# A planner that sorts TensorE's work by when its operands are ready, plus a slack: two attention and two feed-forward layers on one core

## The chip, the cores and the metric

The kernel runs on one core of a Trainium2 chip. The metric is device time in microseconds (us) of one execution, as the median of several. A core has five engines that work in parallel, each through its own list of instructions in order: TensorE (PE, matrix products), VectorE (DVE), ScalarE (ACT), GpSimd (POOL) and SyncE (SP, which here only issues transfers). They wait for each other through semaphores.

## The reference: what is computed

x has 2048 tokens of 640 features. The two layers A and B are each applied twice, A, B, A, B, every time as x = x + layer(layernorm(x)):

```python
# A: 32 heads of 20 features; the tokens in 4 segments of 512, one after the other
q, k, v = x @ wq, x @ wk, x @ wv
p     = softmax(q_s k_s^T * scale + causal mask)      # within segment s
a_mem = phi(q_s) M / (phi(q_s) z + 1e-6)              # M, z: of the segments before
o     = g * a_mem + (1 - g) * (p v_s)
M, z += phi(k_s)^T v_s, sum(phi(k_s))                 # phi(t) = t + 1 if t > 0 else exp(t)
out   = o @ wo
# B
out   = relu(x @ w1) @ w2                             # 640 -> 1728 -> 640
```

The segments of A follow each other through M and z. B works on each token alone, so B of one segment can run beside A of another.

## The kernel before, in words

**Tiling.** All work goes by segments (a, s): a is the first or second pair of layers, s one of the four segments. For each segment TensorE does the following, one 128x128 tile of weights at a time:

- `proj_part` and `proj_v` make q, k and v from the normalised, transposed tokens xnT, by matmuls of 512 or 320 columns (recorded under lines L598 and L601 of the helper `group`, which all whole-array matmuls of projections and B share).
- q and k are copied from PSUM to `stg`, spilled to a scratch tensor in HBM (`spill`, L859) and read back in another layout as `pad`, four heads at 32 partitions' distance (`fill`, L906, four transfers for each pair of head groups).
- `scores` (L1078) multiplies q and k of four heads at once in row tiles of 32 partitions. It goes by rounds: one round fills two two-bank slots of PSUM, ACT takes the exponentials of both (`exps`, L1140, 128x1024 each), which frees the slots. POOL cuts the triangle (`causal`, L1152).
- `apply` (L1172) multiplies the result PT by v in column tiles of 32, copies it to `otu`, transposes it by a transfer (`turn_pair`, into `otk`), and DVE divides (`divide`). `mem_read` (L969) and `mem_write` (L1021) read and update M; the latter needs the transposed phi(k), `phk`, again through a transfer.
- `turn_o` transposes the sum of both parts into `oT`, `out_proj` multiplies by wo, and DVE adds the result to x (`add_half`, L1294). `ln_b` normalises and transposes again, and `ffn` and `ffn_rest` (L1352) do layer B.

All transposes by transfer are issued by `turn` (L631). Spills, fills, transposes and output stores share SP's one list. The results of the whole-array matmuls go through four PSUM banks (`MISC`); `evac` copies them out on ACT or DVE, whichever the planner finds free first.

**What sets the order.** No order is written out by hand. Each step above is a Python generator, a *stream*, that yields one operation (`Op`) after the other: the engine or engines that may do it, an estimate of its time on each, what it waits for, and the buffer that it acquires. `Sched.run` plans the program while it is built. It keeps an estimated time at which each engine is free (`free`) and at which each result is ready (`t`, read through `at`). In each step it looks at the head of every stream, and takes the one with the smallest key:

```python
key = (round(start + late), 0.5 if op.urgent else prio, self.rank[id(st[1])], n)
```

`start` is the estimated start: the later of the engine being free and of every operand being ready, plus `SEM_NS` (60) and, on TensorE, `PE_MARGIN` (80). `late` comes from `_late`. Before the change it is 0 except for operations with a `lag` (the column-tiled `apply` and `ffn_rest`, `COLS_LAG` 1500 ns). Ties go by priority (scores and exponentials first, B last) and then by the segment. Score rounds come to the planner as an `Either`; for them `run` sets `late` to 0.0 itself and doesn't call `_late`:

```python
both, lone = st[2].fn()
if both is not None:
    heads.append((st[0], n, st, self._alts(both), both, 0.0))
```

The chosen operation is appended to its engine's list for good. So on the chip every engine works through a fixed list, and if an operand is late the engine stands, whatever else lies further down. The estimates decide the order alone; the waits are real semaphores.

A transfer's estimated landing is its issue, plus bytes by a rate on one shared DMA clock (`dma_free`), plus a latency: `turn` uses 2400 ns and 270 bytes a ns, a spill 2300, a fill 1500 with 130 bytes a ns.

Of the kernel before, what the change touches and what calls it, by code (L numbers as in the profile page):

```python
# [38 lines left out]
class Prog:  # L39
    def __init__(self, sems):  # L40
        self.ops = {e: [] for e in ENGS}
        self.clk = dict(sems)
        self.cnt = {e: 0 for e in ["act", "dve", "pool", "pe"]}
        self.dcnt = {}
        self.K = {e: {} for e in ENGS}
        self.pos = {e: 0 for e in ENGS}
        self.info = {}
# [109 lines left out]
LONE_NS = 300.0  # L157
SWITCH_NS = 96.0
COLS_LAG = 1500.0
SEM_NS = 60.0  # L160
PE_MARGIN = 80.0
HOLDERS = 1
# [3 lines left out]
class Sched:  # L166


    def __init__(self, prog):
        self.P = prog  # L170
        self.free = {e: 800.0 for e in ENGS}
        self.t = {}
        self.events = {}
        self.streams = []
        self.dma_free = 0.0
        self.rank = {}
        self.mode = "full"

    def add(self, prio, gen):
        self.streams.append([prio, gen, None, None, False])  # L180
        self.rank[id(gen)] = 0
# [4 lines left out]
    def set(self, *key, tks=()):  # L186
        assert key not in self.events, key
        self.events[key] = [t for t in tks if t is not None]
# [35 lines left out]
    def _alts(self, op):  # L224
# [7 lines left out]
        for k, (e, hold, fns, tail) in enumerate(op.alts):  # L232
            m = PE_MARGIN if e == "pe" else 0.0
            if e == "pe" and op.mode != self.mode:
                hold = hold + SWITCH_NS
            start = max([self.at(t) + SEM_NS + m for t in waits], default=0.0)
            start = max(self.free[e], start)
# [3 lines left out]
        return res  # L241

    def _late(self, op):
        if not op.lag or self.mode != "full":
            return 0.0
        waits = op.waits
        if op.acq is not None:
            s = self._pick(op.acq)
            waits = waits + (s.tks if s is not None else [])
        ready = max([self.at(t) for t in waits], default=0.0) + SEM_NS + PE_MARGIN  # L250
        return max(0.0, ready + op.lag - max(ready, self.free["pe"]))

    def run(self):
        while True:
            best = None
            moved = True
            while moved:
                moved = False
                for st in self.streams:
                    had, ended = st[2], st[4]  # L260
                    self._settle(st)
                    moved = moved or st[4] != ended
                    moved = moved or st[2] is not had
            heads = []
            for n, st in enumerate(self.streams):
                if st[4]:
                    continue
                if isinstance(st[2], Op):
                    heads.append((st[0], n, st, self._alts(st[2]), st[2], self._late(st[2])))
                elif isinstance(st[2], Either):  # L270
# [3 lines that stand above are left out]
                    if lone is not None:  # L274
                        heads.append((8, n, st, self._alts(lone), lone, LONE_NS))
            for prio, n, st, alts, op, late in heads:
                ok = []
                for end, start, k, e in alts:
                    if not any(p2 < min(prio, HOLDERS) and st2 is not st
                               and any(e2 == e and s2 + HOLD_TOL[e] < end for _, s2, _, e2 in al2[:1])  # L280
                               for p2, _, st2, al2, _, _ in heads):
                        ok.append((end, start, k))
                if not ok:
                    continue
                end, start, k = min(ok)
                key = (round(start + late), 0.5 if op.urgent else prio, self.rank[id(st[1])], n)
                if best is None or key < best[0]:
                    best = (key, st, end, start, k, op)
            if best is None:
                stuck = [st for st in self.streams if not st[4]]  # L290
                if not stuck:
                    return
                raise RuntimeError("stuck: " + "; ".join(
                    str(getattr(st[2], "key", None) or [s.name for s in getattr(st[2], "slots", [])][:2]) for st in stuck))
            _, st, end, start, k, op = best
            e, hold, fns, tail = op.alts[k]
            if e == "pe":
                self.mode = op.mode
            waits, slot = op.waits, None
            for s in op.take:  # L300
                s.free = False
            if op.acq is not None:
                slot = self._pick(op.acq)
                slot.free = False
                waits = waits + slot.tks
                fns = [(lambda eng, fn=fn, slot=slot: fn(eng, slot), mark) for fn, mark in fns]
            self.P.waits(e, waits)
            self.free[e] = end
            if op.dma is not None:
                tk = self.P.dma(e, fns[0][0], op.dma)  # L310
                self.dma_free = max(self.dma_free, start + 300.0) + tail[1]
                self.t[(id(tk[0]), tk[1])] = max(self.dma_free, end) + tail[0]
                if tail[2]:
                    self.free[e] = max(end, self.dma_free)
                out = tk
            else:
                marks = []
                for fn, mark in fns:
                    tk = self.P.op(e, fn, mark)
                    if tk is not None:  # L320
                        self.t[(id(tk[0]), tk[1])] = end + tail
                        marks.append(tk)
                out = marks[0] if len(marks) == 1 else (marks or None)
            st[2], st[3] = None, ((slot, out) if slot is not None else out,)


def pe(ns, fns, waits=(), acq=None, take=(), mode="full", lag=0.0):
    return Op([("pe", ns, fns, 190.0)], waits, acq=acq, take=take, mode=mode, lag=lag)
# [18 lines left out]
def evac(n, mode, vfn, afn, waits=(), psum=True):  # L347
    return Op([("act", (60.0 if psum else 94.0) + n / 1.2, [(afn, True)], 125.0),
               ("dve", 66.0 + n / (0.96 * mode), [(vfn, True)], 95.0)], waits, urgent=True)
# [12 lines left out]
def bass_interleave_layers__memory_aug_infini_attn__dense_activation_relu__prompt_kernel(  # L362
    nc, A_x, A_wq, A_wk, A_wv, A_wo, A_beta, B_x, B_w1, B_w2, out,
):
    with contextlib.ExitStack() as es:
# [794 lines left out]
        def apply(n):  # L1160
# [9 lines left out]
            for j in range(NJ):  # L1170
                for hh in range(4):
# [3 lines left out]
                        j == NJ - 1 and hh == 3))  # L1175
            OD, tk = yield pe(540.0, fns, mk + vt, acq=MISC, mode="cols", lag=COLS_LAG)
            pt.release(tk)
# [164 lines left out]
        def ffn_rest(b, s):  # L1342
# [6 lines left out]
            for k in range(FC):  # L1349
                for z in range(2):  # L1350
                    for c in range(2):
# [4 lines left out]
                            start=(k == 0), stop=(k == FC - 1)), k == FC - 1 and z == 1 and c == 1))  # L1356
            bk, tk = yield pe(550.0, fns, xtk + w1t, acq=MISC, mode="cols", lag=COLS_LAG)
            th = yield evac(256, 1, lambda e: e.tensor_scalar(hR[:], bk.ap[:, 0:L // 2], 0.0, None, ALU.max),
# [141 lines left out]
```

## Time and profile before

| | |
|---|---|
| median of 8 runs | 567.72 us (566.27 to 570.42) |
| the profiled execution: its own time | 569.41 us |
| the profiled execution: span of its instructions | 567.7 us |
| TensorE (PE) busy | 554.2 us, 98% |
| VectorE (DVE) busy | 412.9 us, 73% |
| ScalarE (ACT) busy | 406.4 us, 72% |
| GpSimd (POOL) busy | 192.4 us, 34% |
| exponentials, L1140 | 320 of 1025 ns |
| granted TensorE clock | full speed in every slice |

The page is of one execution. Its span runs from the first instruction to the last, and its time (569.41) has 1.7 us around that. "Busy" is the union of the instructions' records on an engine. A matmul's record includes its way through the pipeline, so matmuls overlap in the records, and the time from one start to the next is the better measure of what one costs. "Idle before" is the engine's gap before an instruction, and behind the arrow stands what ended it. The chain of waits is followed back from the last instruction through whatever released each one. PEld are the loads of weights, which run beside matmuls.

### The profile page before, as it was taken

How to read it: one execution, taken by the hardware profiler on the slowest of the kernel's cores; microseconds unless marked ns; L12 is line 12 of the kernel's file. 1: busy time of each engine (PE TensorE's matmuls, PEld its weight loads, DVE VectorE, ACT ScalarE, POOL GpSimd, SP SyncE). 2: the span in 40 equal slices, each digit the busy share in tenths (PEclk: the TensorE clock that was granted, in tenths of full speed). 3: DMA queues.
4: the chain of work that ended last, by engine and by line, in shares of the span. 5: the costliest groups of instructions: out<-in, count | busy, mean ns of one | idle time of the engine just before them, and what ended most of it. 6: DMA issues, size and time to landing. Idle time of an engine off the chain costs nothing.

```text
span 567.7 us, 12814 instructions
## 1 busy us (share of the span) xinstructions
PE 554.2 (98%) x5212; PEld 297.0 (52%) x5212; DVE 412.9 (73%) x1064; ACT 406.4 (72%) x512; POOL 192.4 (34%) x302
## 2 busy tenths in 40 slices
PE   7998999999999999999999999999999999999998
PEld 6554554445454545645445545564444553665655
DVE  5957898977989799877587985599856875562202
ACT  5699879889778878978898776688777777213140
POOL 5346344343444344344333442044331433100000
PEclk9999999999999999999999999999999999999999
DMA  8695998835374428472288122861429510432101
GB/s 267 145 219 160 209 210 182 228 70 103 91 140 89 86 57 164 98 106 43 83 156 143 21 51 53 207 99 26 62 74 174 110 44 18 90 69 52 44 0 47
DMA packets 129980, 60.92 MB, mean 107 GB/s; under 512 B 108802, under 2 KB 119810, under 8 KB 129922
## 3 DMA queue, kind: packets, MB, share of 16 engines
q1 hardware_dynamic: 129504, 59.62, 48.9%
q8 instruction: 41, 0.67, 0.5%
q10 hardware_dynamic: 418, 0.49, 0.3%
q14 instruction: 17, 0.14, 0.1%
HBM read 20.57 MB, written 12.85 MB: 59 GB/s over the span
## 4 chain that ended last, share of the span: by engine, by line
PE 76%; DVE 11%; DMA 8%; ACT 2%; SPq 1%; POOL 1%; issue 1%; ACTq 0%
PE ps L601 49%; PE ps L598 10%; PE ps L1078 7%; PE ps L1172 5%; DMA otk<-otu 3%; DVE stats L609 2%; ACT PT L1140 1%; DVE hT L1379 1%; PE ps L1021 1%; PE ps L969 1%; PE ps L1211 1%; DMA pad<-scr 1%; DMA oT<-o_sb 1%; DMA phk<-phs 1%; DVE o_sb L1266 1%; SPq L906 1%
## 5 line engine op out<-in xcount | busy, mean ns | idle before, releaser
L1140 ACT ACTIVATE PT<-ps 128x1024 bf16<-128x1024 f32 x320 | 308.9, 1025 | 69.0 <-PE ps L1078 66.3
L1152 POOL TENSOR_SCALAR_AFFINE_SELECT PT<-PT 128x512 bf16<-128x512 bf16 x256 | 167.0, 671 | 271.4 <-ACT PT L1140 271.3
L601 PE MATMUL ps<-w_r,hT 128*128 128x320 bf16 x768 | 123.5, 299 | 0.0
L601 PE MATMUL ps<-xnT,w_r 128*128 128x512 bf16 x416 | 114.6, 379 | 0.0
L1294 DVE TENSOR_TENSOR x_sb<-x_sb,ps 128x320 bf16<-128x320 bf16 x128 | 60.7, 481 | 69.5 <-PE ps L601 68.9
L601 PEld LDWEIGHTS ps<-w_r,hT 128*128 128x128 bf16 x768 | 72.9, 98 | 33.1 <-issue 5.6
L1078 PE MATMUL ps<-pad 20*128 20x512 bf16 (+3 forms) x1024 | 63.4, 301 | 2.5 <-DMA pad<-scr 1.2
L601 PEld LDWEIGHTS ps<-xnT,w_r 128*128 128x128 bf16 x416 | 39.6, 98 | 42.2 <-issue 3.4
L609 DVE BATCH_NORM_STATS2 stats<-x_sb 128x6 f32<-128x320 bf16 x124 | 55.3, 469 | 2.8 <-DMA x_sb<-in_A_x_dram 2.6
L1379 DVE TENSOR_SCALAR hT<-ps 128x512 bf16<-128x512 f32 x54 | 36.8, 682 | 13.0 <-PE ps L601 12.8
L601 PE MATMUL ps<-wo_r,oT 128*128 128x320 bf16 x256 | 46.2, 299 | 0.0
L1078 PEld LDWEIGHTS ps<-pad 20*128 20x128 bf16 x1024 | 17.9, 92 | 53.1 <-ACT PT L1140 26.5
L1381 ACT ACTIVATE hT<-ps 128x512 bf16<-128x512 f32 x50 | 29.9, 598 | 21.9 <-PE ps L601 21.6
L1172 PE MATMUL ps<-PT,v_aug 128*21 128x128 bf16 (+3 forms) x896 | 40.5, 301 | 0.0
L598 PE MATMUL ps<-xnT,w_r 128*128 128x512 bf16 x104 | 39.6, 381 | 0.3 <-DVE om_sb L980 0.3
L1182 DVE CAST otu<-ps 128x512 bf16<-128x512 f32 x49 | 33.4, 682 | 7.3 <-PE ps L1172 7.1
L601 PE MATMUL ps<-wv_r,xnT 128*128 128x320 bf16 x192 | 36.3, 300 | 0.0
L625 POOL TENSOR_TENSOR rstd<-lnU,mhalf 128x2 f32<-128x2 f32 (+2 forms) x26 | 20.4, 783 | 44.3 <-DVE lnU L621 42.2
L935 ACT ACTIVATE stg<-stg 128x512 bf16<-128x512 bf16 x50 | 31.6, 632 | 4.6 <-DVE rtmp L933 4.4
L601 PE MATMUL ps<-xnT,wk_r 128*128 128x512 bf16 (+1 forms) x128 | 34.8, 366 | 0.0
L601 PE MATMUL ps<-xnT,wq_r 128*128 128x512 bf16 (+1 forms) x128 | 33.6, 366 | 0.0
L655 DVE TENSOR_SCALAR xn_tok<-x_sb,mv,rstd 128x640 bf16<-128x640 bf16 x60 | 30.3, 538 | 2.0 <-POOL rstd L625 1.7
(108 smaller groups left out, 672.0 us busy)
## 6 DMA issues: line engine op xcount, KB each, us to landing
pad<-scr SPq DMA_DIRECT2D x124, 80.0 KB
scr<-stg SPq DMA_DIRECT2D x34, 256.0 KB, 3.3
out_dram<-x_sb SPq DMA_DIRECT2D x16, 160.0 KB, 1.8
w_r<-in_B_w_dram SPq DMA_DIRECT2D x10, 216.0 KB, 2.6
w_r<-in_B_w_dram SPq DMA_DIRECT2D x13, 160.0 KB, 2.8
x_sb<-in_A_x_dram SPq DMA_DIRECT2D x10, 160.0 KB, 3.4
scr<-w_r SPq DMA_DIRECT2D x5, 256.0 KB, 3.3
wv_r<-in_A_wv_dram SPq DMA_DIRECT2D x1, 800.0 KB, 8.7
```

The costliest lines, as they stand in the source:

```text
L598: bk, tk = yield pe(mm_ns(n), [(lambda e, bk, a=a, b=b: e.matmul(bk.ap[:, 0:n] if len(b.shape) == 2 else bk.ap[:, 0:n].rearrange("p (i n) ...
L601: tk = yield pe(mm_ns(n), [(lambda e, k=k, a=a, b=b, bk=bk: e.matmul(bk.ap[:, 0:n] if len(b.shape) == 2 else bk.ap[:, 0:n].rearrange("p (i ...
L609: tk = yield dve(320, 1, lambda e, c2=c2: e.bn_stats(stats6[:, t % 12, c2, :], x_sb[:, t, c2 * 320:(c2 + 1) * 320]), xt)
L655: nm = lambda e, bx, t, k: e.tensor_scalar(bx.ap[:, k * D:k * D + D], x_sb[:, t + k, :], mv[:, t + k, 0:1], rstd[:, t + k:t + k + 1], ALU. ...
L935: te = yield act(512, lambda e, q=q: e.activation(q, q, ACT.Exp), [tr] + p, psum=False)
L1078: fns.append([(lambda e, z=z, j=j, hh=hh, N=N, o=o, sl=sl, q=hh % 2: e.matmul(slot.ap[:, q, o:o + N], sl.ap[32 * hh:32 * hh + DH, z, 0, 12 ...
L1140: tx = yield act(1024, lambda e, dst=dst, src=src: e.activation(dst, src, ACT.Exp, scale=SCALE), sc + pw)
L1152: tm = yield pool(600.0, lambda e, reg=reg: e.affine_select(out=reg, in_=reg, pattern=[[0, 4], [1, 128]], compare_op=ALU.is_ge, fill=0.0, ...
L1172: fns.append((lambda e, OD, j=j, hh=hh: e.matmul(OD.ap[32 * hh:32 * hh + DH + 1, 128 * j:L], VAUG[vx(a, s)][:, j, 4 * g + hh, :], pt.ap[:, ...
L1182: te = yield evac(L, 1, lambda e: e.tensor_copy(dst, OD.ap), lambda e: e.activation(dst, OD.ap, ACT.Copy), [tk] + OTU[0].tks)
L1294: ta = yield dve(320, 1, lambda e: e.tensor_tensor(x_sb[:, t, 320 * hf:320 * hf + 320], x_sb[:, t, 320 * hf:320 * hf + 320], bk.ap[:, 0:32 ...
L1379: th = yield evac(512, 1, lambda e, dc=dc, bk=bk: e.tensor_scalar(hT[:, dc, :], bk.ap[:, :], 0.0, None, ALU.max), lambda e, dc=dc, bk=bk: ...
```

## The change

Three constants are new, and `_late` gets a part for TensorE. It is at work from the point at which the event `("sc",6,4,1)` has been set: the planner has placed the last score round of the seventh pair of head groups, in the second segment of the first layer A. For each operand of the operation (and of the buffer that it would acquire), the estimated time at which it is ready is taken, plus the two margins, plus a slack: 400 ns (`SOFT`) if an engine makes it, 1000 ns (`SOFT_DMA`) if a transfer brings it. If that lies behind the estimated start, the difference is the lateness. It goes into the sort key alone: an operation whose operands have just become ready sorts as if it started later, so others with older operands come first. It isn't kept waiting if there is nothing else, and the start that the planner books is the same. Operations with a `lag` get the larger of both. A set `landed` remembers which results come by a transfer. No instruction, wait, buffer or estimate is changed.

```diff
@@ -157,6 +157,9 @@
 LONE_NS = 300.0
 SWITCH_NS = 96.0
 COLS_LAG = 1500.0
+SOFT = 400
+SOFT_DMA = 1000
+SOFT_FROM = ("sc",6,4,1)
 SEM_NS = 60.0
 PE_MARGIN = 80.0
 HOLDERS = 1
@@ -175,6 +178,7 @@
         self.dma_free = 0.0
         self.rank = {}
         self.mode = "full"
+        self.landed = set()
 
     def add(self, prio, gen):
         self.streams.append([prio, gen, None, None, False])
@@ -241,14 +245,24 @@
         return res
 
     def _late(self, op):
+        late = 0.0
+        if op.alts[0][0] == "pe" and SOFT_FROM in self.events:
+            waits = op.waits
+            if op.acq is not None:
+                s = self._pick(op.acq)
+                waits = waits + (s.tks if s is not None else [])
+            start = max([self.free["pe"]] + [self.at(t) + SEM_NS + PE_MARGIN for t in waits])
+            for t in waits:
+                k = (id(t[0]), t[1])
+                late = max(late, self.t[k] + SEM_NS + PE_MARGIN + (SOFT_DMA if k in self.landed else SOFT) - start)
         if not op.lag or self.mode != "full":
-            return 0.0
+            return late
         waits = op.waits
         if op.acq is not None:
             s = self._pick(op.acq)
             waits = waits + (s.tks if s is not None else [])
         ready = max([self.at(t) for t in waits], default=0.0) + SEM_NS + PE_MARGIN
-        return max(0.0, ready + op.lag - max(ready, self.free["pe"]))
+        return max(late, ready + op.lag - max(ready, self.free["pe"]))
 
     def run(self):
         while True:
@@ -308,6 +322,7 @@
             self.free[e] = end
             if op.dma is not None:
                 tk = self.P.dma(e, fns[0][0], op.dma)
+                self.landed.add((id(tk[0]), tk[1]))
                 self.dma_free = max(self.dma_free, start + 300.0) + tail[1]
                 self.t[(id(tk[0]), tk[1])] = max(self.dma_free, end) + tail[0]
                 if tail[2]:
```

## The prediction, made before the result was known

> **What bounds the kernel now.** I read the page's busy line first, then its chain, then busy time in three stretches of the span, then TensorE's own waits, and last the timeline around the waits. The busy line and the chain say that TensorE is the bound:
>
> ```profile
> PE 554.2 (98%) x5212; PEld 297.0 (52%) x5212; DVE 412.9 (73%) x1064; ACT 406.4 (72%) x512; POOL 192.4 (34%) x302
> ...
> PE 76%; DVE 11%; DMA 8%; ACT 2%; SPq 1%; POOL 1%; issue 1%; ACTq 0%
> ```
>
> TensorE's order in the two built programs is the same for its first 516 pieces of work, up to the apply at 111.6 us. So the change can act only behind that point. The stretches (us busy, instructions):
>
> ```profile
> 0.00:111.60 111.60, 105.53 (x1169) 58.10 (x1170) 89.82 (x247) 92.18 (x124) 48.55 (x85) 1.00 0.83 203
> 111.60:450.00 338.40, 333.80 (x3161) 172.75 (x3155) 273.49 (x701) 270.21 (x331) 127.08 (x191) 1.00 0.49 97
> 450.00:567.70 117.70, 114.89 (x892) 66.13 (x890) 49.61 (x118) 44.04 (x59) 16.77 (x26) 1.00 0.20 48
> ```
>
> The columns are length, then PE, PEld, DVE, ACT, POOL, the clock (1.00 throughout) and DMA. In the middle stretch DVE (273.5) and ACT (270.2) stand at 81% and 80% of 338.4; they have room, TensorE has none. Its waits there:
>
> ```profile
> PE ps L1078 <- DMA pad<-scr: 1.2, 1, 1.2
> PE ps L598 <- DMA oT<-o_sb: 1.1, 1, 1.1
> PE ps L598 <- DMA xnT<-xn_tok: 0.8, 1, 0.8
> PE ps L1021 <- DMA phk<-phs: 0.4, 1, 0.4
> ```
>
> These gaps run from a modelled end, and a matmul's record is longer than its place in the pipeline, so they understate the loss. I count from start to start instead:
>
> ```profile
> 398.77 1.03 PE L601 MATMUL ps<-xnT,w_r 128*128 128x512 bf16 x4
> 400.62 0.31 PE L598 MATMUL ps<-wv_r,xnT 128*128 128x320 bf16 x1 [0.82 <-DMA xnT<-xn_tok]
> ```
>
> Four matmuls of 0.38 us cover 1.03, so they start (1.03 - 0.38)/3 = 0.216 apart. The next should have started at 398.77 + 4 x 0.216 = 399.63 and started at 400.62: 0.99 us lost, not 0.82. The same median steps over the trace are 0.136 for 320 columns, 0.230 for a score round, 0.558 for an apply by columns, and 0.098 more at each change between whole-array, row-tile and column-tile matmuls. They sum to 551.8 us of TensorE work. From the first matmul's start (1.59) to the last one's is 563.05. So 11.3 us are lost to waiting: 4.1 before 111.6 us, **7.2 behind it**. That 7.2 is all the change can win.
>
> It is made of 4.05 for transfers (1.30 pad at 432.07, 1.26 oT at 250.88, 0.99 xnT, 0.50 phk at 294.07), 2.36 in twelve waits of 0.07 to 0.50 for DVE or ACT (0.65 of it four score rounds waiting for L1140), and 0.78 in pieces under 0.06.
>
> [...]during the 0.99 us above no other matmul ran, though work was at hand; so where an operand is late, the place in the list is all that matters. [...]here a change costs 0.098 us against 0.003 between equal matmuls. [...]A spill of this trace issued at 421.08 landed at 423.10, so 2.0; the transposes below take more[...].
>
> **The change, part by part.** The new part of `_late` adds a lateness to the sort key of TensorE operations whose operands would be less than 400 ns (1000 for DMAs) old. It emits no instruction and no wait of its own.
>
> 1. *TensorE work and mode changes.* Both orders have 5,212 matmuls and 394 mode changes (394 x 0.098 = 38.5 us). Cost 0. If grouping had suffered, ten more changes would cost 1.0.
>
> 2. *Transfers.* I summed the measured steps between the last matmul that a transfer depends on and the matmul that needs it, in each order. oT: 12.57 before, 13.95 after; +1.38 against 1.26 lost. xnT: 9.69 and 11.42; +1.73 against 0.99. phk: 14.68 and 15.62; +0.94 against 0.50. All three should go; the queues behind them shift, so I leave 0.2 for them (0 to 1.0). The pad wait is different: score rounds enter the list with lateness 0.0 (the `Either` branch of `run`), and the distance is 9.06 in both. What moves is SP:
>
> ```profile
> 421.08 3.29 SPq L859 DMA_DIRECT2D scr<-stg  x3
> 424.72 1.24 SPq L631 DMA_TRANSPOSE otk<-otu  x1
> 426.05 4.62 SPq L906 DMA_DIRECT2D pad<-scr  x8
> ```
>
> Before: three spills, a transpose of 1.24, fills. Without its 1.30 the score round would stand at 430.77, so the first fill went out 4.72 before it. After: the transpose stands ahead of the third spill. Its apply ends 7.97 us of work ahead of the round (6.90 before); the issue followed 0.85 later, so 7.12 ahead, done at 5.88; the spill's 0.35 and the hand-over make the first fill 5.45 ahead. That is 0.73 sooner: 1.30 becomes 0.57. The third fill was held 1.83 us instead of 0.38; without that nothing is left. I take 0.4 (0 to 1.3).
>
> 3. *A new tight place.* At the segment before the last, the first score round comes 6.58 us of work after the last group that a spill ahead of its fills waits for (9.41 before). With issue 0.83 after the group and 0.40 for the spill, the fills go out 5.35 ahead; from the first fill to landing took 426.05 to 432.03 = 5.98, or 4.5 without the held fill. Loss 0 to 0.6; I take 0.2. The cover is the FFN work in between; with it gone the whole 5.98 would show.
>
> 4. *Engine waits.* For each of 1,242 TensorE pieces behind 111.6 us other than score rounds I took the shortest work distance over a DVE, ACT or POOL operand. Below 1.3 us lie 34 before and 4 after; below 1.4, 49 and 14. Seven of the eight non-score waits in the list lie below 1.43. I take 0.6 of their 1.71 as left (0.2 to 1.7). Score rounds: the four that waited lay 2.08 to 2.10 us behind the round whose exponentials free their banks; the shortest is 2.19 after. 0.1 of 0.65 left (0 to 0.65). Pieces under 0.06: 0.7 of 0.78.
>
> 5. *Moved evictions.* The order of times lets the planner give 39 evictions from DVE to ACT and 29 the other way: ten more on ACT at 598 ns (the L1381 row) is 6.0 us, 82% of the middle stretch instead of 80. They hide under TensorE unless one falls between a score round and its exponentials. Bound: 0, to 10 x 0.2 = 2.0 (0.6 less a typical slack of 0.4: median distance 2.5 against some 2.1 needed). I take 0.3. The tail from 450 us is the same FFN backlog in both.
>
> Sum: left over 0.2 + 0.4 + 0.2 + 0.6 + 0.1 + 0.7 + 0.3 = 2.5 of 7.2; gain 4.7. The profiled execution has span 567.7 and time 569.41, so its time would be 564.7. It is 1.7 above the median 567.72; the gain is the same there: 567.72 - 4.7 = **563.0**. What is late next is TensorE's own work.
>
> **Rivals.** *(a) The waits only move.* Slack is worth nothing if the true lag exceeds it: [...]delayed heads start their chains later. The pad wait, out of the rule's reach, speaks for it; the grown distances speak against. With 1.0 of 7.2 gone net: 566.7, within 0.3% (1.7 us, about what a measurement of this kernel can tell from no change). *(b) The fills come too late; slower.* Place: SP at the last two segment starts, where a transpose now stands ahead of the third spill. If its apply's eviction or buffer is late, spill and fills wait with it, and score rounds and everything behind them on TensorE stand. Price per start: the 1.30 seen, 1.24 for one more transpose, 1.45 for the held fill, 4.0; two starts 8.0, of which 0.6 is counted: 567.72 - 4.7 + 7.4 = 570.4. It decides once the two lose more than 4.7 + 1.7 = 6.4 together. The SP order speaks for it; the first fill's earlier place in item 2 against it. *(c) Nothing is left but small pieces*: 567.72 - 6.5 = 561.2, if the held fill does not recur and DVE is never behind.
>
> **How the numbers follow.** Forecast 563.0: 0.60, own range 561.5 to 565.5. (c) 561.2: 0.15. (a) 566.7: 0.15. (b) 570.4: 0.10. Faster 0.60 + 0.15 = 0.75, same 0.15, slower 0.10. The range 560.5 to 567.2 leaves out (b) and the rims: the low end is all 7.2 gone (560.5), the high end a gain of 0.5.
>
> **What would show it.** Right: in the waits of TensorE behind 111.6 us the oT, xnT and phk rows vanish, pad shrinks below 0.6, start-to-start loss there falls from 7.2 to about 2.5, and PE busy stays near 554. Wrong: a new DMA wait over 1 us (item 3 or b), many short waits on x_sb, otu or v_aug (item 4), score rounds waiting for PT more often than four times (item 5), or more mode changes than I count.

## The result, and the profile after

| | before | after |
|---|---|---|
| median time, us | 568.19 (31 runs) | 564.72 (11 runs) |
| ratio | | 0.9939, 95% interval 0.9927 to 0.9951 |
| the profiled execution: time, span | 569.41, 567.7 | 564.48, 562.7 |
| start-to-start loss ahead of 111.6 us (the prediction's measure) | 4.09 | 3.99 |
| the same behind it | 7.19 | 2.33 |
| mode changes of TensorE | 394 | 394 |

The change made the kernel 3.5 us faster (0.6%; 2.8 to 4.1 by the interval). The forecast was 563.0. The profile after, busy line and chain (line numbers are 15 or so higher than before, L601 is now L616, L1078 L1093, L1140 L1155):

```profile
PE 552.9 (98%) x5212; PEld 296.9 (53%) x5212; DVE 410.2 (73%) x1054; ACT 410.9 (73%) x522; POOL 193.1 (34%) x302
...
PE 82%; DVE 8%; DMA 5%; ACT 2%; SPq 1%; issue 1%; POOL 0%; ACTq 0%
```

TensorE's busy time is the same within 1.3 us, so the work did not change; in the chain TensorE's share rose from 76 to 82% and that of transfers fell from 8 to 5%. The stretches, with the middle one ended at the same place before the end (columns as in the prediction):

```profile
0.00:111.60 111.60, 105.51 (x1170) 57.85 (x1171) 90.25 (x248) 92.32 (x125) 48.37 (x85) 1.00 0.83 203
111.60:445.00 333.40, 332.41 (x3148) 172.47 (x3146) 272.93 (x690) 271.01 (x334) 127.82 (x191) 1.00 0.47 98
445.00:562.70 117.70, 115.00 (x908) 66.54 (x896) 46.97 (x118) 47.55 (x65) 16.91 (x26) 1.00 0.21 48
```

The first and the last stretch stand as they stood (105.5 and 115.0 busy). The middle one is 333.4 long instead of 338.4, and TensorE's gaps in it went from 4.6 to 1.0 us. All that its waits behind 111.6 us still list:

```profile
PE ps L1093 <- ACT PT L1155: 0.2, 1, 0.2
PE ps L613 <- DVE otu L1197: 0.2, 1, 0.2
```

The four rows of transfers that the prediction showed are gone.

**A note on the measure.** The prediction took each step as a median in whole nanoseconds. Over some 4,000 steps that counts fractions of a nanosecond as loss. From here on, steps are means over undisturbed neighbours, the same in all profiles: the loss behind 111.6 us is then 6.55 before and 1.87 after, and pieces under 0.06 us sum to 0.14 and 0.04 instead of 0.78 and 0.50. The expectations of the runs still give losses in the prediction's measure, so their figures stand some 0.6 higher (1.23 for e9, which is 0.63 in the table). Loss is also a subtraction: the time from the first matmul to the last, less the steps that TensorE's own work takes. That the span follows the whole loss is therefore no test. What is measured is where the loss sits and what ended each wait.

### The profile page after: what moved, and what is told of

Its sections match the earlier page's. It is cut to its first block, busy times and chain, and to the rows that moved or that the text cites. A ratio compares the mean times of both kernels' runs of the same rounds, so it can differ in the third digit from the quotient of the medians.

```text
span 562.7 us, 12825 instructions
## 1 busy us (share of the span) xinstructions
PE 552.9 (98%) x5212; PEld 296.9 (53%) x5212; DVE 410.2 (73%) x1054; ACT 410.9 (73%) x522; POOL 193.1 (34%) x302
## 4 chain that ended last, share of the span: by engine, by line
PE 82%; DVE 8%; DMA 5%; ACT 2%; SPq 1%; issue 1%; POOL 0%; ACTq 0%
PE ps L616 53%; PE ps L613 11%; PE ps L1093 8%; PE ps L1187 5%; DMA otk<-otu 2%; DVE stats L624 1%; ACT PT L1155 1%; DVE o_sb L1281 1%; PE ps L984 1%; PE ps L1036 1%; PE ps L1226 1%; DVE x_sb L1309 1%; DMA phk<-phs 1%; PE ps L1367 1%; DVE hT L1394 1%
## 5 line engine op out<-in xcount | busy, mean ns | idle before, releaser
L1155 ACT ACTIVATE PT<-ps 128x1024 bf16<-128x1024 f32 x320 | 309.0, 1026 | 59.6 <-PE ps L1093 53.6
L616 PE MATMUL ps<-w_r,hT 128*128 128x320 bf16 x768 | 124.3, 299 | 0.0
L616 PE MATMUL ps<-xnT,w_r 128*128 128x512 bf16 x416 | 113.6, 379 | 0.0
L616 PEld LDWEIGHTS ps<-w_r,hT 128*128 128x128 bf16 x768 | 72.5, 98 | 33.1 <-issue 5.8
L1093 PE MATMUL ps<-pad 20*128 20x512 bf16 (+3 forms) x1024 | 63.4, 301 | 1.3 <-ACT PT L1155 1.0
L616 PEld LDWEIGHTS ps<-xnT,w_r 128*128 128x128 bf16 x416 | 39.3, 98 | 43.0 <-issue 3.9
L1396 ACT ACTIVATE hT<-ps 128x512 bf16<-128x512 f32 x56 | 33.5, 599 | 22.8 <-PE ps L616 22.1
L616 PE MATMUL ps<-wo_r,oT 128*128 128x320 bf16 x256 | 46.2, 300 | 0.0
L1093 PEld LDWEIGHTS ps<-pad 20*128 20x128 bf16 x1024 | 17.8, 92 | 51.7 <-ACT PT L1155 26.6
L1394 DVE TENSOR_SCALAR hT<-ps 128x512 bf16<-128x512 f32 x48 | 32.7, 683 | 11.7 <-PE ps L616 11.5
L1197 DVE CAST otu<-ps 128x512 bf16<-128x512 f32 x46 | 31.4, 682 | 9.1 <-PE ps L1187 8.9
L616 PE MATMUL ps<-wv_r,xnT 128*128 128x320 bf16 x192 | 36.2, 300 | 0.0
L616 PE MATMUL ps<-xnT,wk_r 128*128 128x512 bf16 (+1 forms) x128 | 34.9, 366 | 0.0
L616 PE MATMUL ps<-xnT,wq_r 128*128 128x512 bf16 (+1 forms) x128 | 33.9, 366 | 0.0
L951 DVE TENSOR_TENSOR phs<-stg,rtmp 128x512 bf16<-128x512 bf16 x50 | 24.0, 480 | 10.2 <-ACT stg L950 9.5
```

Source lines behind the costliest of these rows:

```text
L616: tk = yield pe(mm_ns(n), [(lambda e, k=k, a=a, b=b, bk=bk: e.matmul(bk.ap[:, 0:n] if len(b.shape) == 2 else bk.ap[:, 0:n].rearrange("p (i ...
L1093: fns.append([(lambda e, z=z, j=j, hh=hh, N=N, o=o, sl=sl, q=hh % 2: e.matmul(slot.ap[:, q, o:o + N], sl.ap[32 * hh:32 * hh + DH, z, 0, 12 ...
L1155: tx = yield act(1024, lambda e, dst=dst, src=src: e.activation(dst, src, ACT.Exp, scale=SCALE), sc + pw)
L1197: te = yield evac(L, 1, lambda e: e.tensor_copy(dst, OD.ap), lambda e: e.activation(dst, OD.ap, ACT.Copy), [tk] + OTU[0].tks)
L1394: th = yield evac(512, 1, lambda e, dc=dc, bk=bk: e.tensor_scalar(hT[:, dc, :], bk.ap[:, :], 0.0, None, ALU.max), lambda e, dc=dc, bk=bk: ...
L1396: lambda e, dc=dc, bk=bk: e.activation(hT[:, dc, :], bk.ap[:, :], ACT.Relu), [tk] + HT.tks)
```

## The experiments

Theory 1: the time is TensorE's fixed work plus what it loses to waiting for single late operands, and each slack takes away the waits of its own kind. Rivals: only one of the slacks works (A), or the gain comes from moved evictions or mode changes and not from waits (B). Here are all kernels, with the loss behind 111.6 us split by what was waited for (score rounds apart, for they have no slack):

| kernel | ratio (95%) | span | loss | transfers | DVE, ACT | score rounds | mode changes |
|---|---|---|---|---|---|---|---|
| before | 1 | 567.7 | 6.55 | 4.05 | 1.70 | 0.66 | 394 |
| after | 0.9939 (0.9927 to 0.9951) | 562.7 | 1.87 | 0.18 | 1.15 | 0.50 | 394 |
| e1 slack for transfers alone | 0.9976 (0.9965 to 0.9987) | 565.0 | 4.11 | 0.14 | 2.71 | 1.15 | 392 |
| e2 slack for engines alone | 0.9982 (0.9971 to 0.9994) | 564.7 | 4.24 | 2.92 | 0.07 | 1.29 | 394 |
| e4 later landings, no slack | 0.9951 (0.9932 to 0.9970) | 563.2 | 2.58 | 0.41 | 1.07 | 0.91 | 395 |
| e5 score rounds too | 1.0120 (1.0096 to 1.0145) | 572.7 | 10.85 | 9.73 | 1.11 | 0 | 403 |
| e6 from the first round on | 0.9944 (0.9922 to 0.9966) | 563.2 | 2.27 | 0.35 | 0.54 | 1.41 | 395 |
| e7 both slacks doubled | 0.9927 (0.9905 to 0.9949) | 562.7 | 1.06 | 0 | 0.37 | 0.69 | 394 |
| e9 later landings, engine slack | 0.9911 (0.9889 to 0.9932) | 561.5 | 0.63 | 0 | 0.20 | 0.45 | 390 |

The rest of each loss is in pieces under 0.06. In e5 all but 9.27 is no wait but a slower clock (below). Ratios and their intervals are from all timed runs; span and loss are from one profiled execution each.

**One slack alone: e1 and e2.**

```diff
-SOFT = 400
+SOFT = 0          # e1
-SOFT_DMA = 1000
+SOFT_DMA = 0      # e2
```

> Slack for transfers alone (SOFT 0, SOFT_DMA 1000). The order keeps 33 TensorE pieces with an engine operand less than 1.3 us of work old (34 before, 4 with both slacks), lengthens the oT, xnT and phk distances (14.6, 15.2 and 21.8 us of work against 12.6, 9.7 and 14.7), leaves pad at 9.1, and has 392 mode changes. Theory 1 (the time is TensorE's fixed work plus its start-to-start loss, and each slack removes the waits of its own kind): transfer loss 4.05 to some 0.5, engine and small losses stay near 3.1, so loss 3.6 behind 111.6 us and a span near 564. Rival A (the engine slack does the work, transfers would have landed anyway): loss stays above 5, span 566 or more. Rival B (the gain comes from the moved evictions or from fewer mode changes, not from waits): span and loss do not move together.

> Slack for engines alone (SOFT 400, SOFT_DMA 0). 8 pieces below 1.3 us; oT distance 12.3 (shorter than before by 0.3), xnT 11.8, phk 20.7, pad 15.2; 394 mode changes; 513 ACT instructions, so no evictions move to ACT on balance. Theory 1: engine and small losses fall to some 1.3, pad, xnT and phk waits go because the order moved them apart, the oT wait stays at 1.3 to 1.6; loss 2.9, span near 563.4. Rival A: the same or less, 562.7. If each slack removes waits of its own kind only: transfer losses of 4 stay and the span is 566.

TensorE's waits behind 111.6 us, of e1:

```profile
PE ps L1093 <- ACT PT L1155: 0.8, 1, 0.8
PE ps L984 <- DVE phs L951: 0.7, 1, 0.7
PE ps L984 <- DVE om_sb L995: 0.2, 1, 0.2
PE ps L613 <- DVE v_aug L852: 0.2, 1, 0.2
PE ps L613 <- DVE otu L1197: 0.2, 1, 0.2
```

and of e2:

```profile
PE ps L1036 <- DMA phk<-phs: 1.2, 1, 1.2
PE ps L1093 <- ACT PT L1155: 0.8, 2, 0.4
PE ps L613 <- issue: 0.5, 1, 0.5
PE ps L613 <- DMA oT<-o_sb: 0.4, 1, 0.4
PE ps L1093 <- DMA pad<-scr: 0.3, 1, 0.3
```

The two lists are nearly mirror images. e1 has no row of a transfer left (0.14 us of loss; 4.05 before), and the waits that it lists are all for DVE or ACT. e2 has hardly a wait for DVE or ACT outside score rounds (0.07; 1.70 before) and 2.9 us for transfers. Its row "issue" is one of these: the matmul at 174.98 reads an xnT that landed at 174.89. e1's loss was some 1.1 us larger than expected (the 3.6 expected is 3.0 in this measure): its engine places were no fewer, and they cost 2.71 instead of 1.70, so a place with a small distance is a chance of a wait, not a wait. Score rounds, which have no slack, lost more in both (1.15 and 1.29 for 0.66). e2's transfer loss was twice what I expected, and it stands at other transfers than in the kernel before (the phk wait is at 254.18, not 294.07): I had taken distances that the order happened to lengthen for safety. Each slack alone gives a part (2.4 and 2.3 us less loss, 1.4 and 1.0 us of time). In the profiled executions the two reductions, 4.75 together, are as large as that of both slacks at once (4.68). In the timed runs they aren't: 1.4 and 1.0 make 2.4, and both at once gave 3.5. So that the two simply add is not shown. Rival A is out, for both intervals lie below 1. So is rival B: the engine slack alone moved no evictions to ACT on balance (511 instructions there for 512), kept 394 mode changes, and gained; and ACT has ten instructions more in the changed kernel (522) but eight fewer in e9 (504), which gained too.

**Another remedy for transfers: e4.** The estimate itself is put later, with no slack in the key:

```diff
-SOFT_FROM = ("sc",6,4,1)
+SOFT_FROM = ("never",)
...
-self.t[(id(tk[0]), tk[1])] = max(self.dma_free, end) + tail[0]
+self.t[(id(tk[0]), tk[1])] = max(self.dma_free, end) + tail[0] + (1000.0 if ("sc",6,4,1) in self.events else 0.0)
```

> No slack in the sort key; instead the planner's estimate of every transfer's landing is 1000 ns later from the same point on. Distances: oT 16.1, xnT 11.6, phk 18.2, pad 11.2 us of work; 34 engine places below 1.3 us as before; 395 mode changes. Theory 1: the transfer waits go as with the transfer slack, engine waits stay, loss 3.5, span near 564. Rival: later landings also hold back score rounds, which starves ACT and shows as new waits for PT; span 566 or more.

Transfers lose 0.41, as expected. Engine waits fell too (1.07), which I had not expected with as many short distances as before; I have no experiment on why, and the same caution as for e1 holds. That estimates of landings 1000 ns later take the transfer waits away as the slack does fits with estimates that were too early. It isn't shown that this is all, for the later estimates also reach the score rounds and the other engines, which the slack leaves alone. The score rounds were not starved in general: their 0.91 (0.66 before) is one round at 115.9.

**The exception for score rounds: e5.**

```diff
-heads.append((st[0], n, st, self._alts(both), both, 0.0))
+heads.append((st[0], n, st, self._alts(both), both, self._late(both)))
```

> The slack is asked of score rounds too (the Either branch calls _late instead of passing 0.0). No score round is less than 2.45 us of work behind the round that frees its banks (2.19 with the change, 2.08 before), the pad distance of the last segment grows from 9.1 to 35.6 us; but there are 403 mode changes instead of 394 (+0.9 us), and the last score round ends at 498.4 us of TensorE work instead of 472.5, so that the last out_proj ends at 522.8 and its feed-forward layer begins at 524.4, with no other work to cover the normalisation and transposes between. Theory 1: score and pad waits vanish (0.7 us gained) but 5 to 9 us of standing appear at one place near the end; span 568 to 571, slower than the change. Rival (priority of scores is not what fills the tail; all slack is good): span under 562.

TensorE near the end (start, duration, engine and line; in brackets the idle time and what ended it):

```profile
528.36 0.71 PE L616 MATMUL ps<-wo_r,oT 128*128 128x320 bf16 x4
538.17 0.59 PE L613 MATMUL ps<-xnT,w_r 128*128 128x512 bf16 x1 [9.11 <-DMA xnT<-xn_tok]
538.55 1.91 PE L616 MATMUL ps<-xnT,w_r 128*128 128x512 bf16 x4
540.25 0.63 PE L613 MATMUL ps<-xnT,w_r 128*128 128x512 bf16 x1
...
542.88 1.03 PE L616 MATMUL ps<-xnT,w_r 128*128 128x512 bf16 x4
543.75 0.38 PE L613 MATMUL ps<-xnT,w_r 128*128 128x512 bf16 x1
```

No score round waited any more (0), and TensorE lost 9.27 us in one place: with the last out_proj it had nothing left until the normalised tokens of the last segment had been transposed. In both main kernels a whole segment of feed-forward work lies there (26 us of it before, 25 after), because there the rounds that start each chain are not put off. The time is outside the span that I expected (572.7 for 568 to 571); two terms were missing: the clock, below, and the full length of that chain. Of these kernels only this one is slower than the one before: asked of the head of the chain that ends last, slack uses up the work that covers its tail.

**More of it: e6 and e7.** e6 sets `SOFT_FROM = ("sc",0,0,1)`, e7 `SOFT = 800` and `SOFT_DMA = 2000`.

> The same slacks from the first score round on instead of the seventh pair. The first 111.6 us lose 4.0 us to waiting with the change; 1.6 to 1.9 of that lie before the first score round and are out of reach. Distances: 12 pieces below 1.3 us, pad 10.3, the score round of the segment before the last 9.06, xnT 10.8; 395 mode changes. Theory 1: up to 2 us less loss in the first 112 us, some 0.5 more behind it (xnT and the two fills are as tight as before the change); span 561.5 to 563. Rival: in the first segment transfers run at a share of 0.8 of the engines' time and land later than any slack allows for, so delaying chain heads costs there; span above 563.

> Both slacks doubled (800 and 2000). 2 pieces below 1.3 us and 2 below 1.4 (4 and 14 with the change), longer oT, xnT, phk distances (14.8, 14.1, 24.9), but score rounds, which have no slack, come as close as 1.92 us to the round before (2.19); 394 mode changes. Theory 1: engine and transfer waits nearly vanish, waits of score rounds for exponentials grow from 0.5 to 1 or more; loss 2 to 3 behind 111.6 us, span 562 to 563.5, equal to the change within the noise. Rival (more slack, more gain): span 561.5 or less.

e6 gained nothing over the change: the loss ahead of 111.6 us is the same in both, and score rounds lose 1.41 instead of 0.50, of it 0.83 in one round at 116.1. The span (563.2) is where its rival put it; that late transfers of the first segment are the reason isn't shown. e7's loss is 0.8 lower than the change's, its ratio is lower by 0.0012, and the intervals overlap: no difference that these runs can tell. Its score rounds lost 0.69 and not 1 or more.

**Both remedies together: e9.** e4's edit, now tied to `SOFT_FROM`, and slack 400 for every operand:

```diff
-SOFT_DMA = 1000
+SOFT_DMA = 400
...
-self.t[(id(tk[0]), tk[1])] = max(self.dma_free, end) + tail[0]
+self.t[(id(tk[0]), tk[1])] = max(self.dma_free, end) + tail[0] + (1000.0 if SOFT_FROM in self.events else 0.0)
```

> Landings are estimated 1000 ns later from the same point on, and every operand has the engines' slack of 400. 4 pieces below 1.3 us, oT 16.9, xnT 25.5, phk 24.3, pad 15.8 us of work; 390 mode changes (0.4 us less). Theory 1: each kind of wait has its remedy, loss 2 to 2.5, span 562 to 562.7, as fast as the change. Rival (stacked delays hold the heads of chains back too far): loss above 3.5, span above 563.5.

Its loss is 0.63, less than I expected, and its waits show one row, a score round:

```profile
PE ps L1093 <- ACT PT L1155: 0.2, 1, 0.2
```

To tell it from the change, both ran once more on one chip:

> The changed kernel once more, on the same chip as its best rival version. If its first ratio of 0.9939 holds: 0.993 to 0.995, loss behind 111.6 us 2.3 within 0.5, span 562.7 within 0.6.

> Later landings with the engines' slack once more (loss 1.23, 390 mode changes). Theory 1 says that it beats the change by the difference of the losses, 1.1, and four mode changes, 0.4: ratio lower by 0.0026, near 0.991. If its first ratio was luck of the chip: equal to the change.

The change: 564.83 us, ratio 0.9939 (0.9918 to 0.9960), loss 2.02. e9: 563.62, ratio 0.9925 (0.9900 to 0.9950), loss 0.58. Its median is lower by 1.2 us here (0.8 by the ratios), and its first one (563.37) by 1.35 than that of the change in the result; the losses and four mode changes (0.4) would make 1.8 and 1.6. The intervals overlap, so it is likely faster, not shown to be.

**How much the unchanged program varies: e3, e12, e13.** The slack is never switched on (`SOFT_FROM = ("never",)`).

> The kernel before, built with the changed source and the slack never switched on: instruction for instruction the same program. It shows how far its waits differ from one execution to another. If the profiled execution of before was typical: loss behind 111.6 us 7.2 within 0.5, span 567.7 within 0.6. If it was a long one (its time 569.41 stands above the median of 568.19): loss near 6, span near 566.5, and the true gain of the change is nearer the 3.5 of the timed runs than the 5.0 of the two spans.

> Another look at the unchanged program. The two profiles so far have 7.2 and 7.4 us of loss behind 111.6 us, and times of 569.4 and 569.0, above their medians. If the loss makes the time: an execution nearer 568 shows a loss of some 6, with the same places in the list and smaller waits for transfers. If the time varies for another cause: the same loss at a shorter time.

> As the look before it: loss behind and ahead of 111.6 us and time move together, one us for one us, if the loss makes the time.

| execution of the kernel before | time | loss behind 111.6 us | of it transfers |
|---|---|---|---|
| the profile shown | 569.41 | 6.55 | 4.05 |
| e3 | 569.00 | 6.79 | 3.29 |
| e12 | 568.36 | 5.77 | 3.31 |
| e13 | 569.78 | 7.28 | 3.83 |

From the shortest to the longest the time grew by 1.42 and the loss by 1.51; the two between stand the other way round, the loss by 0.2. The whole time must follow the whole loss, as said above; what the table adds is how much of it lies behind 111.6 us, where the change works. Transfers are waited for at the same four places in all of them, with waits that differ by up to half a us each; e3 and e13 have one wait more, for DVE (last section). e3 alone would have passed for typical, but it was a long execution too. e12 is the one at the median.

## Why the prediction was right, and where its sizes were off

1. *TensorE work and mode changes, cost 0.* Right: 394 and 394, busy 554.2 and 552.9.

2. *Transfers.* The oT, xnT and phk waits went, as their distances said. Landing came 2.05, 1.58 and 1.37 us before the need in the trace after (0.04, 0.05 and 0.05 before); the 0.2 kept for them was not needed. For the pad wait, SyncE after the change:

```profile
419.90 1.24 SPq L646 DMA_TRANSPOSE otk<-otu  x1
421.19 0.57 SPq L874 DMA_DIRECT2D scr<-stg  x1
421.80 2.59 SPq L921 DMA_DIRECT2D pad<-scr  x4
```

The order is that of the prediction, and the first fill goes out 5.23 us ahead of the score round (427.03), near the 5.45 worked out and 0.5 sooner than before. The third fill was held again (1.36 us), and still no wait was left; I had kept 0.4. It is a slim margin: in e2 two other transposes (3.07 us in SyncE's list) came between the fills, and the same round lost 0.40 although its work distance was 15.2 instead of 9.1. So the distance on TensorE alone does not decide this wait; what stands in SyncE's list between the fills does too.

3. *A new tight place*, first score round of the segment before the last: 0.2 taken, 0.18 measured (0.16 in e10).

4. *Engine waits.* Too small: 0.6 of 1.71 taken as left, 1.15 measured (1.49 in e10). Half of it is memory reads, for which "shortest work distance" was the wrong gauge. They share one PSUM bank, which three DVE instructions must free, and those stand in DVE's list among others. In the trace after:

```profile
329.80 0.16 DVE L992 TENSOR_SCALAR rmem<-ps 128x16 f32<-128x16 f32 x1
329.88 0.43 DVE L670 TENSOR_SCALAR xn_tok<-x_sb,mv,rstd 128x640 bf16<-128x640 bf16 x1
...
330.23 0.24 DVE L994 RECIPROCAL rmem<-rmem 128x16 f32<-128x16 f32 x1
...
330.51 0.49 DVE L995 TENSOR_TENSOR om_sb<-ps,rmem 128x320 bf16<-128x320 f32 x1
...
331.06 0.34 PE L984 MATMUL ps<-BD,phs 128*128 128x84 bf16 x3
```

The read at 331.06 lost 0.29 us (0.11 before): its distance fell from 5.4 to 3.2 us of work, well above my 1.3, and DVE was not done. The other half is two waits for `otu` (0.38 and 0.20), whose distances of 0.9 and 0.8 us were below the 1.3 of the count. Score rounds kept 0.50 and not 0.1, in two of them (0.29 at 137.00, 0.22 at 179.13): a shortest distance of 2.19 us instead of 2.08 is no protection when other work stands ahead of the exponentials in ACT's list. At 179.13 these were two evictions (`hT` at 176.04, `otu` at 176.52), at 137.00 an exponential for phi(k), which itself had waited 0.65 us for DVE.

5. *Moved evictions.* ACT's busy time rose by 4.5 us (6.0 worked out) and DVE's fell by 2.7. No wait can be put down to it, unless the evictions ahead of the round at 179.13 are moved ones, which is not known.

By the prediction's own measure 2.33 us of 7.19 was left, where its sum said 2.5. That the two are so close is in part luck, for two errors cancel: transfers cost less (0.18 for 0.8) and engines and score rounds more (1.65 for 0.7, or 1.0 with the 0.3 for evictions); the rest, 0.50 in small pieces where I took 0.7, is mostly rounding of steps and was never a loss.

**The step that was off** is the last of the sum: "the gain is the same there", from an execution 1.7 us above the median to the median. The forecast was 563.0 and the median is 564.7. Of these 1.7 us, 0.5 is the starting point: the median of before was 567.72 in the 8 runs at hand and is 568.19 in 31. The other 1.2 is the gain. In span it was 5.0 (4.7 forecast), in medians 3.5, because the profiled execution of before stands 1.2 above its median and that of the changed kernel 0.2 below. A longer execution of before has longer waits, and there is then more to gain than at the median: the profiled one lost 6.55 behind 111.6 us; e12, at 568.36, lost 5.77, or 0.8 less. The changed kernel's two profiles have times of 564.48 and 564.84 at losses of 1.87 and 2.02. From e12's 5.77 to these is 3.8 to 3.9, near the 3.5 measured. One execution at the median is little to size this by.

Of the rivals, (a) is out, for of 6.55 us 1.87 is left in all, the new waits counted; (b) did not come about; and (c) is what e9 comes near.

## What to carry to other kernels

Where an engine works through a fixed list at 98%, count its loss from start to start and look up each wait's operand; a planner that lets fresh operands age a little in its sort key removed such waits here at no cost in work. Results of engines and of transfers both need an allowance; that they need different ones isn't shown, for no run gave both kinds the same. Leave the heads of the chain that ends last out of it, or the work that should cover its tail is used up early. Scale a gain that is made of waits to the median execution, not to the profiled one.

## What the runs showed of the hardware

*The clock after a pause.* In e5, after the 9.1 us in which TensorE stood, its matmuls of 512 columns started (540.25 - 538.55) / 4 = 0.425 us apart, and behind 542 (543.75 - 542.88) / 4 = 0.217. The stretches of e5:

```profile
530.00:538.00 8.00, 0.00 (x0) 0.00 (x0) 3.71 (x14) 0.00 (x0) 1.39 (x2) 0.58 0.44 82
538.00:542.00 4.00, 3.83 (x27) 1.38 (x27) 0.00 (x0) 0.60 (x1) 0.00 (x0) 0.56 0.02 4
542.00:546.00 4.00, 4.00 (x23) 1.87 (x20) 0.00 (x0) 2.17 (x4) 0.00 (x0) 1.00 0.00 0
```

The granted clock (third column from the right) is 0.56 in the mean of the second stretch, and 1.00 behind it. Cut finer, it is 1.00 from 529.10 to 531.20, 0.50 from 531.30 to 541.40, and 1.00 again from 541.50. The means of the stretches (0.58 and 0.56) follow from these, and so does that of the whole execution, which is 0.991 in all six runs: (572.7 - 10.2 x 0.5) / 572.7. So the clock fell to half 2.2 us after the last matmul had ended (529.07), and it was at full speed again 3.3 us after work began at 538.17. It is one pause: how short a one is enough, and whether the clock comes back as fast after another, isn't shown. The slower steps add 1.6 us to the 9.27 of the pause, which makes the 10.85 of the table.

*A late transpose that reaches TensorE through DVE.* Two of the four profiles of the kernel before (e3 and e13) have one more wait, 1.1 and 1.3 us at 163. In e13:

```profile
160.87 0.35 DVE L1273 RECIPROCAL rden<-otk 128x32 f32<-128x32 bf16 x1 [1.75 <-DMA otk<-otu]
161.14 0.11 DVE L992 TENSOR_SCALAR rmem<-ps 128x16 f32<-128x16 f32 x1
```

The transpose into otk, issued at 154.49, held DVE until 160.87, or 6.4 us later; in the first profile of before one issued at 155.22 had landed after 4.2 and DVE did not wait. The memory read's three instructions stand behind it in DVE's list (161.14, 161.66 and 162.59). No TensorE operand is a transfer there, so no slack for transfers on TensorE sees it. Neither profile of the changed kernel shows this wait; whether the change did that or chance, these runs don't tell.
